# Seven half products per block pair for half of batch 6's first product, and what was moved with it

## The chip, the cores and the metric

The kernel runs on one core of one Trainium2 chip. The metric is the device time of one execution in microseconds, as the median of several runs.

## The reference

Two parts follow each other. A linear attention (cosFormer) on `q`, `k`, `v` of 8 batches, 8 heads, 576 positions, 64 features gives `x` of (8, 576, 512). Then a mixer: a low-rank mix over positions, and a two-layer product over channels.

```python
k_p = phi(k, cos_w, sin_w); q_p = phi(q, cos_w, sin_w)   # relu times cos and sin: 128 features
kv = einsum('bhsf,bhsd->bhfd', k_p, v); z = sum(k_p, axis=2)
attn = einsum('bhsf,bhfd->bhsd', q_p, kv) / (einsum('bhsf,bhf->bhs', q_p, z)[..., None] + 1e-06)
x = attn.transpose(0, 2, 1, 3).reshape(B, S, H * D)       # (8, 576, 512)
h = x.transpose(0, 2, 1) @ U @ V                          # U (576, 32), V (32, 576)
u = x + h.transpose(0, 2, 1)
out = u + maximum(u @ w_ch1, 0.0) @ w_ch2                 # w_ch1 (512, 2048), w_ch2 (2048, 512)
```

## The kernel before

**Tiling.** Per batch, 512 of the 576 positions are four chunks of 128; the other 64 are the tail, and two batches share one tail tile. All matmuls are bf16 with fp32 sums in PSUM, whose eight banks are named `g0 g1 g2 o0 o1 T` and `X` (one tile of two banks). The first product (`u @ w_ch1`, hidden width 2048 as 16 blocks of 128) is "g"; the second (`hid @ w_ch2`) is made of half products `h_ps`.

**Order.** The program is one list, `slots`. A slot is a piece of PE work: a block of the first product (`g1_main`, L566: four matmuls of 512 columns into `g0` or `g1`, then a relu on ACT), a half product (`half_part`, L853: eight matmuls of 256 columns, L882), or a quarter of a tail (`g1_tail`, L700: four blocks, 16 matmuls of 128 columns, "a tail unit"). `put(at, thunk)` hangs other work behind slot number `at`. Nothing reorders afterwards: each engine runs its own instructions in the order in which the program gave them, and waits by semaphore for what it reads or overwrites.

**Stages.** While batch b's first product runs block by block, the second product of batch b-1 is interleaved as two times seven half products (Strassen's seven for eight, with the sums `w2_sum` L789 and `hid_sum` L811), and the attention of batch b+1 is hung beside them by `attention_plan` (L991): `q_prep` and `k_prep` (ACT and DVE), `kv_unit`, five `x_unit`s (L415), `A_unit` (L452), `u_mm` (L468), four `u_add`s (L481), the transposes `utr_dma` (SP's queue), and for odd batches `u_tail` (L488). `PLAN[7]` gives 191 as the base slot of batch 7.

**x unit.** Eight matmuls fill the two banks of `X` (L422), DVE makes the reciprocal of the denominators (L412, L413) and one multiplication for all 8 heads (L432). The next x unit writes the same tile `X`.

**Batch 7's first product** uses seven products per block pair p (block p and block p+8): `g1_cross` (L647) issues product i as two matmuls of 256 columns (L670). X and Y are the halves of one bank, Z half of another; two pairs alternate over `CROSS = [("g0", "g1"), ("g2", "T")]`. The steps of a pair are

- `opened`: products 1 (X) and 2 (Y); P1 = cast of X on ACT; C11 = P1 + Y on DVE
- `second`: products 6 (onto X) and 5 (Z); casts U2 of X and P5 of Z
- `third`: product 7 (onto X); C22 = P5 + X on DVE, relu on ACT
- `closed`: products 3 (onto Z) and 4 (onto X); C12 = U2 + Z on DVE, relu of X on ACT, one relu of the upper half on DVE (L692)

It needs sums of `w_ch1` quarters (`w1_sum`, L610, in the freed tiles of `qst` and `kst`) and of the batch's transposed `u` (`uT_sum`, L631, in the freed tile of `vst`), all on DVE (L608).

**Results of the second product** of batches 5 and 6: ACT casts four of the seven half products to `o_sb`, DVE adds the others (L838), and `half_store` (L935) lets GpSimd add `u_bf` and then stores.

Of the kernel before, what the change touches and what calls it, by code (L numbers as in the profile page):

```python
# [17 lines left out]
def kernel(  # L18
# [396 lines left out]
    def x_unit(b, c, tag, bufs):  # L415
        x_alloc(b)
        n = P if c < 4 else TS
        rows = slice(0, P) if c < 4 else tail(b)
        acc = ps.tile([P, 2, 512], FP32, tag=tag, bufs=bufs, name="x_ps")
        for h in range(H):  # L420
            g, i = divmod(h, 4)
            nc.tensor.matmul(  # L422
                out=acc[:, g, i * E : i * E + E],
                lhsT=qT_of(b, c, h),
                rhs=kv_sb[b][:, h, :],
                start=(i == 0),
                stop=(i == 3),
            )
        view = acc[rows, :, 0 : 4 * E].rearrange("p g (i e) -> p g i e", e=E)
        rec = pool.tile([P, 2, 4], FP32, tag="rec", bufs=2, name="rec")  # L430
        recip(rec[rows], view[:, :, :, D])
        nc.vector.tensor_tensor(  # L432
            out=x_of(b, c, rows).rearrange("p (g i d) -> p g i d", g=2, d=D),
            in0=view[:, :, :, 0:D],
            in1=rec[rows].unsqueeze(3).to_broadcast([n, 2, 4, D]),
            op=ALU.mult,
        )

    def A_of(b):
        return A_sb[b % 4]  # L440
# [24 lines left out]

    va = {}

    def u_mm(b, *spare):  # L468
        if b not in u_bf:
            u_bf[b] = pool.tile([P, 4, 4, P], BF16, tag="u_bf", bufs=3, name="u_bf")  # L470
        va[b] = four_banks(*spare)
        for c in range(4):
            for j in range(4):
                rows = slice(j * R, j * R + R)
                nc.tensor.matmul(  # L475
                    out=va[b][j][:, c * P : c * P + P], lhsT=V_bf[rows, c, :],
                    rhs=A_of(b)[rows, :], start=(c == 0), stop=(c == 3),
                    tile_position=(j * R, 0),
                )
# [5 lines left out]
            in1=va[b][j].rearrange("p (c n) -> p c n", c=4), op=ALU.add,  # L485
        )

    def u_tail(pr, *spare):  # L488
        u_tl[pr] = pool.tile(
            [P, DM], BF16, tag="k_p" if pr == 3 else "u_tl", bufs=1, name="u_tl"  # L490
        )
        vt = four_banks(*spare)
        for i in range(2):
            for j in range(4):
                rows = slice(j * R, j * R + R)
                nc.tensor.matmul(
                    out=vt[j][tail(i), 0:P], lhsT=V_tl[rows, :],
                    rhs=A_of(2 * pr + i)[rows, :], start=True, stop=True,
                    tile_position=(j * R, i * TS),
                )  # L500
        for j in range(4):
            ns = slice(j * P, j * P + P)
            nc.vector.tensor_tensor(
                out=u_tl[pr][:, ns], in0=x_tl[:, ns], in1=vt[j][:, 0:P], op=ALU.add
            )
# [4 lines left out]

    def uTt_alloc(pr):
        if pr not in uT_tl:
            uT_tl[pr] = pool.tile([P, 4, P], BF16, tag="uT_tl", bufs=1, name="uT_tl")

    def utr_dma(b, c0, c1):
        if c0 < 4:
# [113 lines left out]

    def uT_sum(b, i):  # L631

        if i == 1:
            t = pool.tile([P, 4, 2, 2, P], BF16, tag="vst", bufs=1, name="uT_s")
            for n in range(4):
                uT_s[b, n + 1] = t[:, n]
        x, y = {
            1: lambda: (uT_quarter(b, 0, 1), uT_quarter(b, 0, 0)),
            2: lambda: (uT_quarter(b, 1, 1), uT_s[b, 1]),
            3: lambda: (uT_quarter(b, 1, 1), uT_quarter(b, 0, 1)),  # L640
            4: lambda: (uT_quarter(b, 1, 0), uT_s[b, 2]),
        }[i]()
        diff(uT_s[b, i], x, y)
# [3 lines left out]
    def g1_cross(b, p, i):  # L647

        if (b, p) not in cross:
            if b not in hid:
                hid[b] = pool.tile([P, NJ, 512], BF16, tag="hid", bufs=2, name="hid")
            xy, z = [
                psum.tile([P, 512], FP32, tag=tag, bufs=1, name="c_ps") for tag in CROSS[p % 2]
            ]
            cross[b, p] = {"X": xy[:, 0:256], "Y": xy[:, 256:512], "Z": z[:, 0:256]}
        w = cross[b, p]
        cs = slice(p * P, p * P + P)
        to, lhs, rhs, first = {  # L660
            1: lambda: ("X", W1[0], uT_quarter(b, 0, 0), True),
            2: lambda: ("Y", W1[1], uT_quarter(b, 1, 0), False),
            3: lambda: ("Z", w1_s[4], uT_quarter(b, 1, 1), False),
            4: lambda: ("X", W1[3], uT_s[b, 4], False),
            5: lambda: ("Z", w1_s[1], uT_s[b, 1], True),
            6: lambda: ("X", w1_s[2], uT_s[b, 2], False),
            7: lambda: ("X", w1_s[3], uT_s[b, 3], False),
        }[i]()
        for d in range(2):
            nc.tensor.matmul(  # L670
                out=w[to].rearrange("p (c t) -> p c t", c=2), lhsT=lhs[:, d, cs],
                rhs=rhs[:, d], start=(first and d == 0), stop=(d == 1),
                skip_group_check=not first,
            )

    def g1_join(b, p, i):
# [7 lines left out]
        if i == "C11":  # L684
            diff(top[:, lo], w["P1"], w["Y"], ALU.add)
        elif i == "C22":
            diff(low[:, hi], w["P5"], w["X"], ALU.add)
            relu(low[:, hi], low[:, hi])
        elif i == "C12":
            diff(top[:, hi], w["U2"], w["Z"], ALU.add)  # L690
            relu(low[:, lo], w["X"])
            V_.tensor_scalar(out=top, in0=top, scalar1=0.0, scalar2=None, op0=ALU.max)  # L692
        else:
            if (b, "kept") not in cross:
                cross[b, "kept"] = pool.tile([P, 2, 3, 256], FP32, tag="q_pT", bufs=1, name="kept")
            n = ("P1", "U2", "P5").index(i)
            w[i] = cross[b, "kept"][:, p % 2, n]
            cast(A_, w[i], w["Z" if i == "P5" else "X"])
# [274 lines left out]
    def spare(at):  # L973
# [11 lines left out]
        4: (100, (-20, 1, V_, V_), (-13, 2, A_, V_), -12, (-9, -4, -4)),  # L985
        5: (127, (-24, 2, A_, A_), (-14, 2, A_, V_), (-14, -8, -5), (-8, -4, -4)),
        6: (157, (-23, 2, A_, A_), (-14, 2, A_, V_), (-14, -8, -6), (-8, -4, -4)),
        7: (191, (-24, 2, A_, A_), (-14, 2, A_, V_), (-14, -12, -10), ()),
    }

    def attention_plan(b):  # L991
# [39 lines left out]
            else:  # L1031
                put(4 + (3 * n) // 2, x_unit, c, "X", 1)
        a_at = 15 - b if b < 4 else 14
        put(a_at, A_unit, tag=True)
        odd = b % 2 == 1


        def two(at):
            return [T1, ("s", 1)] if at >= 88 else [spare(at)] * 2

        plan.append((w + a_at + 2, lambda: u_mm(b, *two(w + a_at + 2))))
        for j in range(4):
            put(a_at + 2 + j + (2 if b > 4 and j > 1 else 0), u_add, j)
        put(a_at + 3, utr_dma, 0, 2)
        put(a_at + (7 if b > 4 else 5), utr_dma, 2, 4)
        if odd:
            plan.append(
                (w + a_at + 9, lambda: u_tail(b // 2, *two(w + a_at + 9)))
            )
# [283 lines left out]
    def g1(b, j):  # L1333
        return lambda: g1_main(b, j)
# [22 lines left out]
    for b in range(3, B - 1):  # L1357
# [4 lines left out]
        for n in range(2):  # L1362
            for i7 in range(7):
# [4 lines left out]
        if b % 2:  # L1368
            tail_slots(b // 2)
        if b == 3:  # L1370
            tail_out(b // 2)

    at = len(slots)
    b7 = B - 1
    for i, half, sl in (
        (1, 0, -4), (1, 1, -3), (3, 0, -3), (3, 1, -2), (2, 0, -1), (2, 1, 21), (4, 0, 22), (4, 1, 25),
    ):
        put(at - 30 + sl, lambda i=i, half=half: w1_sum(i, half))
    for i in range(4):
        put(at - 4 + i, lambda i=i: uT_sum(b7, i + 1))  # L1380
    sums(b7 - 1, 0, (at, at + 1, at + 6))
    sums(b7 - 1, 1, (at + 13, at + 15, at + 19))

    def opened(p):
        g1_cross(b7, p, 1)
        g1_cross(b7, p, 2)
        g1_join(b7, p, "P1")
        g1_join(b7, p, "C11")

    def second(p):  # L1390
        g1_cross(b7, p, 6)
        g1_cross(b7, p, 5)
        g1_join(b7, p, "U2")
        g1_join(b7, p, "P5")

    def third(p):
        g1_cross(b7, p, 7)
        g1_join(b7, p, "C22")

    def closed(p):  # L1400
        g1_cross(b7, p, 3)
        g1_cross(b7, p, 4)
        g1_join(b7, p, "C12")

    def group(p, first, then):
        def go():
            if p < 8:
                first(p)
            if p > 0:
                then(p - 1)  # L1410

        return go

    groups = [
        group(p, *fs) for p in range(9) for fs in ((opened, third), (second, closed))
    ]
    halfs = [(n, i7) for n in range(2) for i7 in range(7)]
# [8 lines left out]
    for i, go in enumerate(groups):  # L1426
        slots.append(go)
        if i < 14:
            n, i7 = halfs[i]
            slots.append(lambda n=n, i7=i7: half_part(b7 - 1, n, i7, "with g"))  # L1430
            if i7 > 4:
                put(len(slots), lambda n=n, i7=i7: half_store(b7 - 1, n, i7 - 5))
        else:
            slots.append(lambda j=i - 14: tail_cross(j))
    at = len(slots)
# [76 lines left out]
```

## Time and profile before

| | |
|---|---|
| median of 3 runs | 294.66 us (294.53 to 294.97) |
| profiled execution | 294.26 us, span of its instructions 292.5 us |
| PE busy | 284.3 us, 97% of the span |
| DVE, ACT, GpSimd busy | 203.6, 166.9, 55.8 us |
| granted TensorE clock | 0.998 |
| 210.58 to 240.19 us (batch 6's first product) | PE 29.35, DVE 19.40, ACT 13.41, POOL 5.54 us busy |
| 240.19 to 243.66 us (start of batch 7's) | PE 2.78, DVE 3.40, ACT 1.92, POOL 2.09 us busy |

A row of the timeline gives start, duration, engine, line, operation, what it writes and reads, and in brackets the idle time ahead of it with what ended it. Rows of one engine that overlap are counted once in busy times. A group's row gives busy time, the mean of one in ns, and the idle time ahead of the group with its releasers. The chain of waits names, for each stretch of the span, what the end of the program hung on.

### The profile page before, as it was taken

Reading aid. Unit: us, or ns where it says so; the run is one execution under the profiler, and the core shown is the slowest. Engines: PE = TensorE matmul, PEld = TensorE weight load, DVE = VectorE, ACT = ScalarE, POOL = GpSimd, SP = SyncE. Lnnn points to the kernel's source line nnn. Section 1 sums busy time; section 2 is a strip of 40 time slices with the busy share of each in tenths; the row PEclk is TensorE's granted clock in tenths of the full one; section 3 lists DMA queues with packets and bytes.
Section 4 is the critical chain, followed back from the end, with each engine's and each line's share of the span. In section 5 each row is a group of like instructions: output and inputs, shape, how many; then the busy total and the mean of one; then the engine's idle time right before and its main releaser. Section 6 shows DMA issues by size and latency. Waiting matters only on the chain.

```text
span 292.5 us, 7212 instructions
## 1 busy us (share of the span) xinstructions
PE 284.3 (97%) x2884; PEld 191.8 (66%) x2920; DVE 203.6 (70%) x484; ACT 166.9 (57%) x340; POOL 55.8 (19%) x92
## 2 busy tenths in 40 slices
PE   8999999999999999999999999999999999999994
PEld 4675564447545446676767667766776667889883
DVE  5977855496875697556547793778827687865773
ACT  2955742276882767577736765298753445567210
POOL 6520500000020004202300501040202331302330
PEclk9999999999999999999999999999999999999999
DMA  7999999999998989998799939974800321101023
GB/s 226 304 254 251 275 160 222 205 318 228 340 194 175 294 212 259 240 315 237 147 250 265 242 88 280 231 266 92 215 0 4 110 68 59 50 24 72 2 94 125
DMA packets 90949, 54.07 MB, mean 185 GB/s; under 512 B 58564, under 2 KB 87620, under 8 KB 90916
## 3 DMA queue, kind: packets, MB, share of 16 engines
q1 hardware_dynamic: 84420, 43.94, 60.2%
q0 software_dynamic: 6304, 9.47, 14.6%
q8 instruction: 23, 0.38, 0.5%
q10 hardware_dynamic: 192, 0.20, 0.2%
q14 instruction: 10, 0.08, 0.1%
HBM read 36.86 MB, written 9.44 MB: 158 GB/s over the span
## 4 chain that ended last, share of the span: by engine, by line
PE 90%; DMA 3%; ACT 2%; DVE 2%; issue 1%; ACTq 0%; DVEq 0%
PE g_ps L576 31%; PE h_ps L882 26%; PE o_ps L750 11%; PE gt_ps L710 5%; PE c_ps L670 4%; PE kv_ps L347 3%; PE x_ps L422 3%; DMA qst<-in_q_dram 2%; DVE uT_s L608 1%; PE a_ps L445 1%; PE h_ps L750 1%; PE g_ps L593 1%; DMA uT<-u_bf 1%; PE va_ps L475 1%; PE t_ps L365 1%
## 5 line engine op out<-in xcount | busy, mean ns | idle before, releaser
L576 PE MATMUL g_ps<-uT,w_bf 128*128 128x512 bf16 x408 | 103.5, 379 | 1.3
L585 ACT ACTIVATE hid<-g_ps 128x512 bf16<-128x512 f32 x112 | 65.8, 599 | 64.2 <-PE g_ps L576 63.8
L576 PEld LDWEIGHTS <-w_bf 128*128 128x128 bf16 x434 | 40.9, 98 | 36.7
L882 PEld LDWEIGHTS <-hid 128*128 128x128 bf16 x480 | 45.4, 98 | 9.6
L882 PE MATMUL h_ps<-w_bf,hid 128*128 128x256 bf16 x288 | 37.1, 273 | 0.0
L750 PE MATMUL o_ps<-w_bf,hid 128*128 128x512 bf16 x122 | 29.4, 379 | 0.4 <-issue 0.2
L882 PE MATMUL h_ps<-w_s,S 128*128 128x256 bf16 x208 | 26.5, 273 | 0.0
L131 POOL CAST v_ext<-vst 128x512 bf16<-128x512 f32 (+1 forms) x23 | 15.2, 687 | 57.4 <-DMA vst<-in_v_dram 26.8
L838 DVE TENSOR_TENSOR o_sb<-o_sb,h_ps 128x256 f32<-128x256 f32 (+1 forms) x36 | 15.5, 433 | 15.1 <-PE h_ps L882 9.9
L882 PE MATMUL h_ps<-w_s,hid 128*128 128x256 bf16 x192 | 24.9, 273 | 0.0
L483 DVE TENSOR_TENSOR u_bf<-x_bf,va_ps 128x512 bf16<-128x512 bf16 x27 | 17.7, 680 | 8.3 <-PE va_ps L475 4.7
L838 POOL TENSOR_TENSOR o_sb<-o_sb,u_bf 128x512 f32<-128x512 f32 x10 | 12.1, 1205 | 57.5 <-DVE o_sb L838 43.8
L882 PEld LDWEIGHTS <-S 128*128 128x128 bf16 x208 | 19.9, 98 | 4.4
L838 DVE TENSOR_TENSOR o_sb<-u_bf,h_ps 128x256 f32<-128x256 bf16 x28 | 11.7, 417 | 14.3 <-PE h_ps L882 14.2
L941 POOL DMA_DIRECT2D out_dram<-o_sb x16 | 9.9, 619 | 54.0 <-DVE o_sb L838 51.2
L750 PEld LDWEIGHTS <-hid 128*128 128x128 bf16 x128 | 11.5, 98 | 12.2
L710 PE MATMUL gt_ps<-uT_tl,w_bf 128*128 128x128 bf16 x256 | 16.1, 219 | 0.0
L432 DVE TENSOR_TENSOR x_bf<-x_ps,rec 128x512 bf16<-128x512 f32 x22 | 15.2, 691 | 0.8
L710 PEld LDWEIGHTS <-w_bf 128*128 128x128 bf16 x256 | 14.9, 98 | 0.8
L306 ACT ACTIVATE k_p<-kst,cosw 128x512 bf16<-128x512 f32 x20 | 14.2, 713 | 0.1
L608 DVE TENSOR_TENSOR hid<-kept,c_ps 128x256 bf16<-128x256 f32 x24 | 9.4, 418 | 6.6 <-PE c_ps L670 3.5
L306 ACT ACTIVATE q_p<-qst,sinw 128x512 bf16<-128x512 f32 x18 | 12.6, 709 | 1.7 <-DMA qst<-in_q_dram 1.7
(188 smaller groups left out, 429.0 us busy)
## 6 DMA issues: line engine op xcount, KB each, us to landing
qst<-in_q_dram SPq DMA_DIRECT2D x14, 512.0 KB, 6.0
kst<-in_k_dram SPq DMA_DIRECT2D x14, 512.0 KB, 6.6
vst<-in_v_dram SPq DMA_DIRECT2D x12, 512.0 KB, 6.8
out_dram<-o_sb POOLq DMA_DIRECT2D x19, 256.0 KB, 3.7
out_dram<-o_sb SPq DMA_DIRECT2D x16, 256.0 KB, 2.5
w_bf<-in_moe_w_ch_dram POOLq DMA_DIRECT2D x7, 512.0 KB, 13.7
qst<-in_q_dram SPq DMA_DIRECT2D x2, 640.0 KB, 13.1
kst<-in_k_dram SPq DMA_DIRECT2D x2, 640.0 KB, 7.1
```

The costliest lines, as they stand in the source:

```text
L131: eng.tensor_copy(out=o, in_=i)
L306: nc.scalar.activation(out=o, in_=i, func=AF.Relu, bias=0.0, scale=w)
L432: nc.vector.tensor_tensor(out=x_of(b, c, rows).rearrange("p (g i d) -> p g i d", g=2, d=D), in0=view[:, :, :, 0:D], in1=rec[rows].unsqueez ...
L483: nc.vector.tensor_tensor(out=u_bf[b][:, j, :, :], in0=x_bf[b][:, :, ns], in1=va[b][j].rearrange("p (c n) -> p c n", c=4), op=ALU.add,)
L576: nc.tensor.matmul(out=g_ps.rearrange("p (c t) -> p c t", c=4), lhsT=w1_bf[:, d, j * P : j * P + P], rhs=uT[b][:, d, :, :], start=(d == 0) ...
L585: nc.scalar.activation(out=hid[b][:, j, :], in_=g_ps, func=AF.Relu, bias=0.0, scale=1.0)
L608: V_.tensor_tensor(out=o, in0=x, in1=y, op=op)
L670: nc.tensor.matmul(out=w[to].rearrange("p (c t) -> p c t", c=2), lhsT=lhs[:, d, cs], rhs=rhs[:, d], start=(first and d == 0), stop=(d == 1 ...
L710: nc.tensor.matmul(out=g_ps[:, jj, :], lhsT=w1_bf[:, d, j * P : j * P + P], rhs=uT_tl[pr][:, d, :], start=(d == 0), stop=(d == 3),)
L750: nc.tensor.matmul(out=o[:, cols], lhsT=lhs[:, j, c * P : c * P + P], rhs=w2_bf[:, j, cols], start=(j == 0), stop=(j == NJ - 1),)
L838: eng.tensor_tensor(out=o, in0=x, in1=y, op=ALU.add)
L882: nc.tensor.matmul(out=acc, lhsT=lhs[:, j, :], rhs=rhs[:, j, :], start=(j == 0 and at is not None), stop=(j == 7), skip_group_check=at is ...
```

## The change

1. For batch 6, block pairs 4 to 7 of the first product are made by the seven products; pairs 0 to 3 stay plain. Three banks serve: X and Y of a pair in `g0` or `g1` in turn, and one bank `T` for Z, its halves in turn. `kept` lies in the tile of `q_p`. Batch 6 gets its own four `uT_s` sums.
2. Of the four tail units of pair 2, two stay before batch 6's first product; units 2 and 3 come behind it, in the two banks of `X`. Batch 7's base slot goes from 191 to 189 (its `qtr_dma` keep their slots).
3. As `T` is taken, `u_mm` and `u_tail` of batch 7 are cut: three of four column groups first, the fourth later, alone in `X`.
4. In batch 7's x units of the four chunks DVE does heads 0 to 3, ACT heads 4 to 7 (four scalings); batch 7's `A_sb` cast goes from DVE to ACT, its bank from the tagged one to `g2`.
5. The halves of `w1_sum` get other slots: six ahead of batch 6's first product (before five), two within it (before three).
6. The `half_store`s of batch 5's second half are put eight and nine slots later.

```diff
@@ x_unit
+        gs = 1 if b == B - 1 and c < 4 else 2
         nc.vector.tensor_tensor(
-            out=x_of(b, c, rows).rearrange("p (g i d) -> p g i d", g=2, d=D),
...
+        for i in range(4 * (2 - gs)):
+            nc.scalar.activation(
+                out=x_of(b, c)[:, (4 + i) * D : (5 + i) * D], in_=view[:, 1, i, 0:D],
+                func=AF.Copy, bias=0.0, scale=rec[:, 1, i : i + 1],
+            )
@@ u_mm (u_tail alike)
-    def u_mm(b, *spare):
+    def u_mm(b, *spare, js=range(4)):
-        va[b] = four_banks(*spare)
+        va.setdefault(b, {}).update(zip(js, four_banks(*spare)))
         for c in range(4):
-            for j in range(4):
+            for j in js:
@@ g1_cross
+            if b < B - 1:
+                if "Z" not in cross:
+                    cross["Z"] = psum.tile([P, 512], FP32, tag="T", bufs=1, name="z_ps")
+                xy = psum.tile([P, 512], FP32, tag=("g0", "g1")[p % 2], bufs=1, name="c_ps")
+                z = cross["Z"][:, 256 * (p % 2) : 256 * (p % 2) + 256]
@@ PLAN, attention_plan
-        7: (191, (-24, 2, A_, A_), (-14, 2, A_, V_), (-14, -12, -10), ()),
+        7: (189, (-24, 2, A_, A_), (-14, 2, A_, V_), (-12, -10, -8), ()),
+        if b == B - 1:
+            put(a_at, A_unit, "s", 1, A_)
...
+            plan.append((w + a_at + 2, lambda: u_mm(b, ("s", 1), js=(0, 1, 2))))
+            plan.append((w + a_at + 4, lambda: u_mm(b, js=(3,))))
...
+                plan.append((w + a_at + 9, lambda: u_tail(b // 2, ("s", 1), js=(0, 1, 2))))
+                plan.append((w + a_at + 10, lambda: u_tail(b // 2, js=(3,))))
@@ the slots of batch 6's first product
+        elif b % 2:
+            slots.extend(lambda pr=b // 2, j=j: g1_tail(pr, j) for j in range(2))
...
+    def beside_g(b, m):
+        n, i7 = halfs[m]
+        slots.append(lambda: half_part(b, n, i7, "with g"))
+        if i7 > 4:
+            later = {5: 8, 6: 9}[i7] if (b, n) == (b6 - 1, 1) else 0
+            put(len(slots) + later, lambda: half_store(b, n, i7 - 5))
...
     for i, half, sl in (
-        (1, 0, -4), (1, 1, -3), (3, 0, -3), (3, 1, -2), (2, 0, -1), (2, 1, 21), (4, 0, 22), (4, 1, 25),
+        (1, 1, -8), (2, 1, -6), (3, 1, -4), (1, 0, -3), (4, 1, -2), (3, 0, -1), (2, 0, 11), (4, 0, 23),
     ):
-        put(at - 30 + sl, lambda i=i, half=half: w1_sum(i, half))
+        put(at + sl, lambda i=i, half=half: w1_sum(i, half))
+    for i in range(4):
+        put(at + 1 + i, lambda i=i: uT_sum(b6, i + 1))
+    units = [g1(b6, j) for p in range(3) for j in (p, p + 8)] + [g1(b6, 3)]
+    units.append(lambda: [g1_main(b6, 11), opened(b6, 4)])
+    units.append(crossed((second, b6, 4)))
+    for p in range(5, 8):
+        units.append(crossed((opened, b6, p), (third, b6, p - 1)))
+        units.append(crossed((closed, b6, p - 1), (second, b6, p)))
+    units.append(crossed((third, b6, 7)))
+    slots += units[0:2]
+    for m in range(14):
+        beside_g(b6 - 1, m)
+        slots.append(units[2 + m])
...
+    slots.append(lambda: tail_late(2))
+    slots.append(crossed((closed, b6, 7)))
+    slots.append(lambda: tail_late(3))
```

More of the change, by code (lines that the diff above doesn't have):

```diff
@@ L431, in x_unit @@
         recip(rec[rows], view[:, :, :, D])
+        gs = 1 if b == B - 1 and c < 4 else 2
         nc.vector.tensor_tensor(
-            out=x_of(b, c, rows).rearrange("p (g i d) -> p g i d", g=2, d=D),
-            in0=view[:, :, :, 0:D],
-            in1=rec[rows].unsqueeze(3).to_broadcast([n, 2, 4, D]),
+            out=x_of(b, c, rows)[:, 0 : gs * 256].rearrange("p (g i d) -> p g i d", g=gs, d=D),
+            in0=view[:, 0:gs, :, 0:D],
+            in1=rec[rows, 0:gs].unsqueeze(3).to_broadcast([n, gs, 4, D]),
             op=ALU.mult,
         )
+        for i in range(4 * (2 - gs)):
[3 more added lines that the diff above has]
+            )
     def A_of(b):
@@ L486, in u_add, with u_tail @@
         )
[L488 to L492, printed above, removed]
+    def u_tail(pr, *spare, js=range(4)):
+        if pr not in u_tl:
+            u_tl[pr] = pool.tile(
+                [P, DM], BF16, tag="k_p" if pr == 3 else "u_tl", bufs=1, name="u_tl"
+            )
+        vt = dict(zip(js, four_banks(*spare)))
         for i in range(2):
-            for j in range(4):
+            for j in js:
                 rows = slice(j * R, j * R + R)
@@ L500, in u_tail @@
                 )
-        for j in range(4):
+        for j in js:
             ns = slice(j * P, j * P + P)
@@ L512, in uTt_alloc @@
         if pr not in uT_tl:
-            uT_tl[pr] = pool.tile([P, 4, P], BF16, tag="uT_tl", bufs=1, name="uT_tl")
+            uT_tl[pr] = pool.tile(
+                [P, 4, P], BF16, tag="x_bf" if pr == 3 else "uT_tl", bufs=1, name="uT_tl"
+            )
     def utr_dma(b, c0, c1):
@@ L631, in uT_sum @@
     def uT_sum(b, i):
-        if i == 1:
-            t = pool.tile([P, 4, 2, 2, P], BF16, tag="vst", bufs=1, name="uT_s")
+        if not uT_s:
+            t = pool.tile([P, 2, 4, 2, 2, P], BF16, tag="vst", bufs=1, name="uT_s")
             for n in range(4):
-                uT_s[b, n + 1] = t[:, n]
+                for m in range(2):
+                    uT_s[B - 2 + m, n + 1] = t[:, m, n]
         x, y = {
@@ L653, in g1_cross @@
                 hid[b] = pool.tile([P, NJ, 512], BF16, tag="hid", bufs=2, name="hid")
-            xy, z = [
-                psum.tile([P, 512], FP32, tag=tag, bufs=1, name="c_ps") for tag in CROSS[p % 2]
-            ]
+            if b < B - 1:
[3 more added lines that the diff above has]
+                z = cross["Z"][:, 256 * (p % 2) : 256 * (p % 2) + 256]
+            else:
+                xy, z = [
+                    psum.tile([P, 512], FP32, tag=tag, bufs=1, name="c_ps")
+                    for tag in CROSS[p % 2]
+                ]
             cross[b, p] = {"X": xy[:, 0:256], "Y": xy[:, 256:512], "Z": z[:, 0:256]}
@@ L694, in g1_join @@
             if (b, "kept") not in cross:
-                cross[b, "kept"] = pool.tile([P, 2, 3, 256], FP32, tag="q_pT", bufs=1, name="kept")
+                cross[b, "kept"] = pool.tile(
+                    [P, 2, 3, 256], FP32, tag="q_pT" if b == B - 1 else "q_p", bufs=1,
+                    name="kept",
+                )
             n = ("P1", "U2", "P5").index(i)
@@ L1033, in attention_plan @@
         a_at = 15 - b if b < 4 else 14
[L1034 removed]
+        if b == B - 1:
+            put(a_at, A_unit, "s", 1, A_)
+        else:
+            put(a_at, A_unit, tag=True)
         odd = b % 2 == 1
@@ L1039, in two @@
             return [T1, ("s", 1)] if at >= 88 else [spare(at)] * 2
-        plan.append((w + a_at + 2, lambda: u_mm(b, *two(w + a_at + 2))))
+        if b == B - 1:
+            plan.append((w + a_at + 2, lambda: u_mm(b, ("s", 1), js=(0, 1, 2))))
+            plan.append((w + a_at + 4, lambda: u_mm(b, js=(3,))))
+        else:
+            plan.append((w + a_at + 2, lambda: u_mm(b, *two(w + a_at + 2))))
         for j in range(4):
@@ L1046, in attention_plan @@
         if odd:
-            plan.append(
-                (w + a_at + 9, lambda: u_tail(b // 2, *two(w + a_at + 9)))
-            )
+            if b == B - 1:
+                plan.append((w + a_at + 9, lambda: u_tail(b // 2, ("s", 1), js=(0, 1, 2))))
+                plan.append((w + a_at + 10, lambda: u_tail(b // 2, js=(3,))))
+            else:
+                plan.append((w + a_at + 9, lambda: u_tail(b // 2, *two(w + a_at + 9))))
             put(a_at + 10, utr_dma, 4, 5)
@@ L1356 @@
     alone = len(slots)
-    for b in range(3, B - 1):
+    for b in range(3, B - 2):
         at = len(slots)
@@ L1367, with opened, second @@
                 slots.append(g1(b, 2 + 7 * n + i7))
-        if b % 2:
+        if b == 3:
             tail_slots(b // 2)
-        if b == 3:
             tail_out(b // 2)
+        elif b % 2:
+            slots.extend(lambda pr=b // 2, j=j: g1_tail(pr, j) for j in range(2))
+    b6, b7 = B - 2, B - 1
+    def opened(b, p):
+        g1_cross(b, p, 1)
+        g1_cross(b, p, 2)
+        g1_join(b, p, "P1")
+        g1_join(b, p, "C11")
+    def second(b, p):
+        g1_cross(b, p, 6)
+        g1_cross(b, p, 5)
+        g1_join(b, p, "U2")
+        g1_join(b, p, "P5")
@@ new lines, in third, with closed, crossed, go @@
+    def third(b, p):
+        g1_cross(b, p, 7)
+        g1_join(b, p, "C22")
+    def closed(b, p):
+        g1_cross(b, p, 3)
+        g1_cross(b, p, 4)
+        g1_join(b, p, "C12")
+    def crossed(*steps):
+        def go():
+            for f, b, p in steps:
+                f(b, p)
+        return go
+    halfs = [(n, i7) for n in range(2) for i7 in range(7)]
+    def beside_g(b, m):
[4 more added lines that the diff above has]
+            put(len(slots) + later, lambda: half_store(b, n, i7 - 5))
@@ L1373 @@
     at = len(slots)
-    b7 = B - 1
+    sums(b6 - 1, 0, (at, at + 1, at + 3))
+    sums(b6 - 1, 1, (at + 13, at + 15, at + 19))
     for i, half, sl in (
-        (1, 0, -4), (1, 1, -3), (3, 0, -3), (3, 1, -2), (2, 0, -1), (2, 1, 21), (4, 0, 22), (4, 1, 25),
+        (1, 1, -8), (2, 1, -6), (3, 1, -4), (1, 0, -3), (4, 1, -2), (3, 0, -1), (2, 0, 11), (4, 0, 23),
     ):
-        put(at - 30 + sl, lambda i=i, half=half: w1_sum(i, half))
+        put(at + sl, lambda i=i, half=half: w1_sum(i, half))
@@ L1379, with tail_late @@
+    tail23 = {}
+    def tail_late(j):
+        if j == 2:
+            tail23["t"] = ps.tile([P, 2, 512], FP32, tag="X", bufs=1, name="gt_ps")
+        g1_tail(2, j, tail23["t"][:, j - 2, :].rearrange("p (j t) -> p j t", j=4))
+    slots.append(lambda: tail_late(2))
+    slots.append(crossed((closed, b6, 7)))
+    slots.append(lambda: tail_late(3))
+    at = len(slots)
     for i in range(4):
         put(at - 4 + i, lambda i=i: uT_sum(b7, i + 1))
-    sums(b7 - 1, 0, (at, at + 1, at + 6))
-    sums(b7 - 1, 1, (at + 13, at + 15, at + 19))
@@ L1384, in opened @@
[L1384 to L1403, printed above, removed]
-    def group(p, first, then):
[L1406 to L1412, printed above, removed]
+    sums(b6, 0, (at, at + 1, at + 6))
@@ L1414 @@
+    sums(b6, 1, (at + 13, at + 15, at + 19))
+    def group(p, first, then):
+        return crossed(*([(first, b7, p)] if p < 8 else []), *([(then, b7, p - 1)] if p else []))
     groups = [
@@ L1416 @@
     ]
-    halfs = [(n, i7) for n in range(2) for i7 in range(7)]
     def tail_cross(j):
@@ L1428 @@
         if i < 14:
[L1429 to L1432, printed above, removed]
+            beside_g(b6, i)
         else:
```

## The prediction

> **What bounds the kernel now.** I read the page's busy shares first, then its chain, then the chain in order of time from 205 to 275 us, the timeline of 199 to 250 us, and last the groups by form for the prices.
>
> ```profile
> PE 284.3 (97%) x2884; PEld 191.8 (66%) x2920; DVE 203.6 (70%) x484; ACT 166.9 (57%) x340; POOL 55.8 (19%) x92
> PE 90%; DMA 3%; ACT 2%; DVE 2%; issue 1%; ACTq 0%; DVEq 0%
> ```
>
> PE sets the end, so work that PE no longer does is gained only if PE gets no new gap. The chain in order of time shows the stage that the change rebuilds (first product of batch 6, 210.58 to 240.19 us, "stage 6") and the handover to batch 7 ("stage 7"):
>
> ```profile
> 210.58 0.22 PE g_ps L576
> ...
> 226.09 0.86 PE g_ps L576 x4
> 226.96 0.39 PE a_ps L445 x20
> 227.35 0.98 PE h_ps L882 x8
> ...
> 235.25 2.73 DMA uT<-u_bf
> ...
> 238.58 3.39 DVE uT_s L608 x3
> 241.97 0.34 DVE hid L608
> 242.31 0.04 issue
> 242.35 0.60 PE c_ps L670 x4
> ```
>
> Up to 234 us the pieces are all PE's: sixteen blocks of 0.87, fourteen half products of 0.87, and the attention units of batch 7 fill 29.6 us without a gap. At the handover the chain leaves PE: `u_bf`'s transpose, the four `uT_s` sums, a join, then PE at 242.35. The half product before it began at 240.62 and issues for 0.87, to 241.49: PE lost 0.86 there. Why the sums were late stands in the timeline:
>
> ```profile
> 238.30 1.26 POOL L838 TENSOR_TENSOR o_sb<-o_sb,u_bf 128x512 f32<-128x512 f32 x1 [8.93 <-DVE o_sb L838]
> 238.58 1.26 DVE L608 TENSOR_TENSOR uT_s<-uT,uT_s 128x512 bf16<-128x512 bf16 x1
> 240.10 1.87 DVE L608 TENSOR_TENSOR uT_s<-uT,uT_s 128x512 bf16<-128x512 bf16 x1
> 240.50 1.17 POOL L838 TENSOR_TENSOR o_sb<-o_sb,u_bf 128x512 f32<-128x512 f32 x1
> ```
>
> A sum of 0.42 alone took 1.26 and 1.87, and both ended 0.3 after a GpSimd add. Prices come from these groups:
>
> ```profile
> L1288 ACT ACTIVATE x_bf<-x_ps,rec 128x64 bf16<-128x64 f32 x24 | 5.5, 325 | 7.7 <-DVE rec L412 7.6
> L483 DVE TENSOR_TENSOR u_bf<-x_bf,va_ps 128x512 bf16<-128x512 bf16 x27 | 17.7, 680 | 8.3 <-PE va_ps L475 4.7 <-PE side L475 2.3 <-ACT hid L585 1.3
> L608 DVE TENSOR_TENSOR hid<-kept,c_ps 128x256 bf16<-128x256 f32 x24 | 9.4, 418 | 6.6 <-PE c_ps L670 3.5 <-ACT kept L129 3.1
> ```
>
> Back to back they cost less than their durations, because they overlap: by their starts in the timeline, 0.60 for a DVE operation of 0.68, 0.33 for one of 0.42, 0.27 for an ACT cast of 0.38, 0.49 for the 0.60 relu, and 0.205 for a 64-wide ACT scaling (eight took 1.75). A reader starts 0.20 after PE's last matmul is issued; PE resumes 0.05 after a DVE or ACT result.
>
> **Gains.** Four block pairs go from 8 matmuls of 512 columns (two pieces of 0.867, 1.73) to 14 of 256 (8 in 0.87, so 1.52): 0.21 each, 0.86. Tail units 2 and 3 (0.93 each: all four took 3.73 from 206.85) only change place, but now stand between the last `uT` transposes and stage 7. `u_bf` is done early enough for them to cover the transpose's 2.73 and most of the sums, so the 0.86 gap goes, down to 0.05. Together 1.67.
>
> **Costs.** They are waits, found by laying the built program's instruction order (each wait names its instruction) against these prices. T is the end of the `opened(4)` step.
>
> 1. x units. ACT now scales heads 4 to 7. It waits for DVE's half of the same unit, and the next unit's matmuls into tile X wait for ACT. From a unit's start: matmuls to 0.26, `rec` 0.46, reciprocal 0.66, DVE half (L1089 form, 0.41) 0.89 to 1.29, scalings 1.37 to 2.30. PE returns to X after 0.26 + 0.87 + 0.87 = 2.00 and stands until 2.35. Twice (the third has `opened(4)` between): 0.70. Below: 0, if the rows overlap more; above: 0.9.
>
> 2. A unit. It moves from behind a 0.87 block to behind `second(4)`, 0.43. DVE's queue before it: C11(4) waits for the P1 cast, which stands behind a relu on ACT (relu from T-0.23, cast T+0.26 to 0.64), so C11 starts at T+0.72; then a `hid` sum (T+1.05), `rec` (1.65), reciprocal, DVE half of x (2.09 to 2.49), ACT scalings (2.57 to 3.50). PE: x unit to T+0.26, half product to 1.13, `second(4)` held by C11 to 1.19, then to 1.62, 16 A matmuls to 1.93, and the last wait for 3.55. Stall 1.6, and 0.1 at `second(4)`. Bounds 1.0 (without the sum ahead) and 2.1.
>
> 3. The shared Z bank. Product 5 of pair p+1 waits for C12(p), since both halves of Z are one bank. PE has only products 4 and 6 in between after product 3 (0.65 from the half product's end to product 5); DVE is in order. For pair 5 it must, after the half product ends, do its `o_sb` add (from +0.20), `u_add` 1 (+0.53), a `hid` sum (+1.13), C12 (+1.73 to +2.15): PE starts at +2.20, stall 1.55. For pair 6, from the end e of `opened(6)`: PE has product 7, a half product, products 3, 4 and 6, to e+1.74; DVE has C11(6) from e+0.50 (its cast ends at 0.42), C22 0.83, `u_add` 2 and 3 at 1.16 and 1.76, C12 2.36 to 2.78: stall 1.1. For pair 7: one `o_sb` add and C12, ready at 1.00 against 0.65: 0.35. Sum 3.0; bounds 2.2 and 3.6 (one 0.60 operation more or less, with a little). Behind the waiting product on PE stand the A and U matmuls and every later half product; for them wait `u_add` and the transposes.
>
> Before, `c_ps` has one row of this kind, 0.69 behind `DVE hid`: X and Y of a pair share a bank, and a write into X waits for a read of Y. The Trainium skill ("PSUM — Partial Sum Buffer", bank collisions) says to guard PSUM by bank and not by address. By addresses alone the 3.0 would fall away. Row and rule agree against the change.
>
> 4. Late tail units. Unit 3 writes the two-bank tile that ACT still reads for unit 2: 0.20 + 0.60 + 0.05 against 0.43 of products 3 and 4, so 0.4; the split tail matmuls of `u_tail` wait 0.1 for two adds. Sum 0.5 (0.2 to 0.7).
>
> Covered: the six early `w_ch1` sums (0.60 each) and batch 6's first `hid` sums end by about 211 us on DVE, and the first half product that needs one starts at 215.4; without that cover each costs 0.6. Preparation of batch 7 moves two slots earlier on ACT and DVE: `qst` had landed at about 184, and its first use moves from 190.4 to 188.7. SP's order is unchanged; its `uT` transposes land 5 us before need. The moved GpSimd adds still wait only for their own `o_sb`, and nothing in the program holds them until the later slot, so I give that move nothing either way.
>
> Sum: 0.7 + 1.6 + 0.1 + 3.0 + 0.5 = 5.9 lost, 1.67 gained, +4.2. The profiled execution took 294.26 (span 292.5), so 298.5; that is 0.4 under the median of 294.66, which goes to 298.9.
>
> **Rivals.**
> Faster: DVE and ACT keep up and PE sees none of these waits. For it: DVE is busy 19.4 of 29.6 us in stage 6, ACT 13.4, and before no gap shows there. Against: an average hides an in-order queue that has to answer within 0.65. Time 294.66 - 1.7 = 292.9; it decides if the new gaps sum to less than 1.7.
> No change: the gaps come to 1.1 to 2.3, the time to 294.1 to 295.2.
> Slower by less: DVE runs ahead in the gaps it causes, and terms 1 to 4 go to their low ends, 0 + 1.0 + 2.2 + 0.2 = 3.4, so +1.7 and 296.4.
> Slower by more: the two adds of batch 5's second half start after the last `o_sb` steps, right where the `uT_s` sums of batch 7 are due. If they hold DVE there as in the rows above (1.26 - 0.42 and 1.87 - 0.42, 2.3 in all) and 0.6 of it is covered, it is +5.9 and 300.6. The Trainium skill ("SBUF — State Buffer", Who interferes with whom) calls the port that DVE's two-input operations share with GpSimd an exclusive lock. The stretched rows agree.
> The change doesn't do what it says: the GpSimd adds do not move at all, as above; that is in the forecast.
>
> **How the numbers follow.** Forecast 0.70, less slow 0.12, slower by more 0.07, faster 0.07, no change 0.04. The range goes from the low ends (296.4) to the more-case with a little above (300.8). A measurement of this kernel can tell about 0.2%, 0.6 us, from no change. Faster 0.07, same 0.04, slower 0.89.
>
> **What would show it.** PE gaps in the timeline at the second and third x unit (0.35), before the last A matmul (1.6, released by ACT `x_bf`), before product 5 of pairs 5 to 7 (1.55, 1.1, 0.35, released by DVE `hid`), before the last late tail unit (0.4). The handover gap of 0.86 should be near zero, and the tail of the kernel (from stage 7's second pair on) should last as long as before. I am wrong if product 5 starts without a gap, or if the stretch from batch 6's first block to the second `opened` of stage 7 (before 210.58 to 243.66, 33.1) takes under 36 us, where 33.1 + 1.9 (the moved tails) - 1.7 + 5.9 = 39.2 is forecast.

## The result and the profile after

The changed kernel takes 299.88 us in the median of 6 runs (299.57 to 300.95); the kernel before, beside it on the same chip, took 294.68. The ratio is 1.0174, with a 95% interval of 1.0152 to 1.0197: slower by 5.2 us, where 4.2 were forecast. The profiled execution took 299.85 us with a span of 298.1, which is 5.6 above the span of before; the terms below are held against that 5.6. In the text TensorE, VectorE, ScalarE and GpSimd are the PE, DVE, ACT and POOL of the rows.

The busy shares and the chain's shares, of the page after:

```profile
PE 288.3 (97%) x2944; PEld 194.5 (65%) x2944; DVE 209.1 (70%) x503; ACT 172.4 (58%) x369; POOL 55.0 (18%) x92
PE 86%; DVE 5%; ACT 4%; DMA 2%; issue 1%; ACTq 0%; DVEq 0%
```

TensorE's share stands at 97% as before, so the busy line tells almost nothing. The second line does: TensorE carries 86% of the chain, before it was 90%; VectorE and ScalarE together have gone from 4% to 9%. The work that sets the end now leaves TensorE at several places. Which ones, TensorE's waits between 208 and 250 us say (what waited, for whom: us in total, how often, the longest):

```profile
PE z_ps L687 <- DVE hid L617: 2.6, 3, 1.5
PE a_ps L451 <- ACT x_bf L440: 0.6, 2, 0.4
PE x_ps L422 <- ACT x_bf L440: 0.5, 2, 0.2
PE a_ps L451 <- DVE x_bf L433: 0.4, 1, 0.4
PE gt_ps L730 <- ACT hid_tl L737: 0.2, 1, 0.2
```

In the same view before there was one row, 0.7 of `c_ps` behind `hid` at the handover; it is gone. This view counts from the modelled end of the last matmul, so each wait costs TensorE's queue some 0.1 to 0.2 more than it shows. Counted from issue to issue, as the forecast did, the timeline gives the price: eight matmuls of 256 columns take 0.87, two take 0.22, and what lies between the end of that and the next start is lost. The rows of the longest waits:

```profile
219.52 0.42 PE L422 MATMUL x_ps<-kv,q_pT 128*128 128x65 bf16 x8 [0.24 <-ACT x_bf L440]
227.92 0.22 PE L451 MATMUL a_ps<-x_bf,U_bf 128*32 128x128 bf16 x1 [0.19 <-ACT x_bf L440]
231.36 0.38 PE L687 MATMUL c_ps<-uT_s,w_s 128*128 128x256 bf16 x2
233.27 0.38 PE L687 MATMUL z_ps<-uT_s,w_s 128*128 128x256 bf16 x2 [1.53 <-DVE hid L617]
...
236.93 0.38 PE L687 MATMUL c_ps<-uT_s,w_s 128*128 128x256 bf16 x2
238.23 0.38 PE L687 MATMUL z_ps<-uT_s,w_s 128*128 128x256 bf16 x2 [0.93 <-DVE hid L617]
```

Where the chain left TensorE for the longest time, in order of time:

```profile
224.61 0.42 ACT kept L129
...
225.05 0.42 DVE hid L617
225.47 0.60 DVE S L844
226.07 0.09 DVE rec L412
...
226.19 0.21 DVE rec L413
...
226.42 0.43 DVE x_bf L433
...
226.94 0.94 ACT x_bf L440 x4
...
227.92 0.22 PE a_ps L451
...
230.76 0.60 DVE u_bf L489
231.36 0.33 DVE o_sb L858
231.69 0.60 DVE u_bf L489
232.28 0.60 DVE hid L844
232.89 0.34 DVE hid L617
...
233.27 0.38 PE z_ps L687 x2
```

The first half is `A_unit` standing behind the whole row of cast, C11, `hid` sum, reciprocal, multiplication and four scalings: its 20 matmuls hold TensorE from 226.05 to 228.07, 2.02 where they took 0.39 before. The second half is the shared Z bank: product 5 of pair 5 waits until VectorE has done two `u_add`s, an `o_sb` add and a `hid` sum and has read C12 out of the other half of that bank.

### The profile page after: what moved, and what is told of

It reads as the page before. It is cut to its first block, busy times and chain, and to the rows that moved or that the text cites. A ratio compares the mean times of both kernels' runs of the same rounds, so it can differ in the third digit from the quotient of the medians.

```text
span 298.1 us, 7359 instructions
## 1 busy us (share of the span) xinstructions
PE 288.3 (97%) x2944; PEld 194.5 (65%) x2944; DVE 209.1 (70%) x503; ACT 172.4 (58%) x369; POOL 55.0 (18%) x92
## 4 chain that ended last, share of the span: by engine, by line
PE 86%; DVE 5%; ACT 4%; DMA 2%; issue 1%; ACTq 0%; DVEq 0%
PE g_ps L585 28%; PE h_ps L902 25%; PE o_ps L770 10%; PE c_ps L687 5%; PE gt_ps L730 4%; PE kv_ps L347 3%; PE x_ps L422 3%; DMA qst<-in_q_dram 2%; ACT x_bf L440 1%; DVE hid L617 1%; PE h_ps L770 1%; PE a_ps L451 1%; PE g_ps L602 1%; DVE uT_s L617 1%; DVE x_bf L433 1%
## 5 line engine op out<-in xcount | busy, mean ns | idle before, releaser
L585 PE MATMUL g_ps<-uT,w_bf 128*128 128x512 bf16 x402 | 97.3, 379 | 0.0
L594 ACT ACTIVATE hid<-g_ps 128x512 bf16<-128x512 f32 x104 | 61.1, 600 | 53.7 <-PE g_ps L585 53.0
L585 PEld LDWEIGHTS <-w_bf 128*128 128x128 bf16 x402 | 37.7, 98 | 34.6 <-DMA w_bf<-in_moe_w_ch_dram 0.3
L770 PE MATMUL o_ps<-w_bf,hid 128*128 128x512 bf16 x128 | 30.1, 379 | 0.0
L617 DVE TENSOR_TENSOR hid<-kept,c_ps 128x256 bf16<-128x256 f32 x32 | 12.6, 418 | 13.0 <-ACT kept L129 8.8
L730 PEld LDWEIGHTS <-w_bf 128*128 128x128 bf16 x256 | 15.1, 98 | 1.1 <-issue 0.4
L433 DVE TENSOR_TENSOR x_bf<-x_ps,rec 128x512 bf16<-128x512 f32 (+1 forms) x22 | 14.1, 643 | 0.8
L129 ACT ACTIVATE kept<-c_ps 128x256 f32<-128x256 f32 x32 | 11.4, 382 | 4.7 <-PE c_ps L687 4.2
```

The source lines that it names most:

```text
L433: nc.vector.tensor_tensor(out=x_of(b, c, rows)[:, 0 : gs * 256].rearrange("p (g i d) -> p g i d", g=gs, d=D), in0=view[:, 0:gs, :, 0:D], i ...
L585: nc.tensor.matmul(out=g_ps.rearrange("p (c t) -> p c t", c=4), lhsT=w1_bf[:, d, j * P : j * P + P], rhs=uT[b][:, d, :, :], start=(d == 0) ...
L594: nc.scalar.activation(out=hid[b][:, j, :], in_=g_ps, func=AF.Relu, bias=0.0, scale=1.0)
L617: V_.tensor_tensor(out=o, in0=x, in1=y, op=op)
L730: nc.tensor.matmul(out=g_ps[:, jj, :], lhsT=w1_bf[:, d, j * P : j * P + P], rhs=uT_tl[pr][:, d, :], start=(d == 0), stop=(d == 3),)
L770: nc.tensor.matmul(out=o[:, cols], lhsT=lhs[:, j, c * P : c * P + P], rhs=w2_bf[:, j, cols], start=(j == 0), stop=(j == NJ - 1),)
```

## The experiments

In the expectations "before" is the kernel before, run beside the experiment on the same chip. All kernels below but e3, e6, e9 and e11 start from the changed one. The chips differ between experiments, so a difference between two of them is given by their medians and, where it matters, also by their ratios to before. Two profiles can also differ ahead of batch 6's first block, where the kernels do the same: by 0.78 between before and e6 (210.41 and 211.19). Where traces are compared, the count starts at that block.

**e1: x units wholly on VectorE.**

```diff
-        gs = 1 if b == B - 1 and c < 4 else 2
+        gs = 2
```

> The changed kernel (299.88 us), with batch 7's x units wholly on DVE again; the A_sb cast stays on ACT. Theory of waits: the two gaps of 0.39 before the second and third x unit go, and the wait of the last A matmuls shrinks from 1.55 to about 0.8, because one DVE multiplication of 0.69 takes the place of 0.42 on DVE and then 0.93 on ACT: 1.5 less, 298.4 us. Rival (the half products themselves cost more, waits are a symptom): no change, 299.9 us.

Measured: 298.48 us, ratio 1.0131 (1.0118 to 1.0144). Against the changed kernel that is 1.3 us won back by the ratios, 1.4 by the medians. The rows of `x_ps` waiting for `x_bf` are gone, and `A_unit` has one gap instead of three; TensorE's timeline of e1:

```profile
226.59 0.24 PE L451 MATMUL a_ps<-x_bf,U_bf 128*32 128x128 bf16 x4 [0.70 <-DVE x_bf L433]
231.96 0.38 PE L687 MATMUL z_ps<-uT_s,w_s 128*128 128x256 bf16 x2 [1.53 <-DVE hid L617]
```

So the split of the multiplication costs all of term 1 (0.78 measured) and a little under half of term 2: `A_unit` still holds TensorE 0.90 too long (225.47 to 226.76, less 0.39) where it was 1.63, behind C11 and the `hid` sum, and 0.23 comes back ahead of `second(4)`. The Z wait next to it has not changed at all (1.53 in both).

**e2: a second bank for Z.** Odd pairs put Z in `g2`; for that, V times A is cut in two and two column groups.

```diff
...
-                z = cross["Z"][:, 256 * (p % 2) : 256 * (p % 2) + 256]
+                z = psum.tile([P, 512], FP32, tag=("T", "g2")[p % 2], bufs=1, name="z_ps")
...
```

> The changed kernel, with a bank of its own for Z of the odd pairs (g2); to free it, u_mm and u_tail of batch 7 are cut two and two within X, the second halves one slot later. Theory of waits: product 5 no longer waits for C12, so the gaps of 1.69, 1.08 and 0.35 go, 3.1 in all; the cut two and two costs up to 0.3 in other places: 296.8 to 297.2 us. Rival (the half products themselves cost more): 299.9 us. A second rival: DVE is simply full, so the 3.1 comes back as gaps at other joins, 299 to 300 us.

Measured: 296.89 us, ratio 1.0084 (1.0069 to 1.0099): by the medians 3.0 won back, by the ratios 2.7; from batch 6's first block to the end of the span it is 86.3 (from 209.29) where the changed kernel took 89.4 (from 208.66), so 3.1. No `z_ps` row is left among TensorE's waits; product 5 of pair 5 (`z_ps`) follows product 6 (`c_ps`) at its normal pace, 0.22 later:

```profile
231.98 0.38 PE L685 MATMUL c_ps<-uT_s,w_s 128*128 128x256 bf16 x2
232.20 0.38 PE L685 MATMUL z_ps<-uT_s,w_s 128*128 128x256 bf16 x2
```

VectorE's queue holds the same operations in both kernels, so the queue alone does not cost the 3.1: it costs because TensorE has to wait for a read of the other half of the bank. A full VectorE, the second rival, would have brought the gaps back elsewhere; only the handover grew, from 0.27 to 0.39. Whether the wait belongs to the bank or to the tile that held both halves is not shown, as e2 separates both at once.

**e3 and e9: the late tail units alone**, in the kernel before (batch 7's base slot at 189, `uT_tl` of pair 3 in the tile of `x_bf`).

```diff
+        elif b % 2:
+            slots.extend(lambda pr=b // 2, j=j: g1_tail(pr, j) for j in range(2))
...
+    slots.append(lambda: g1_tail(2, 2))
+    slots.append(tail_x)
```

> The kernel before, with the late tail units alone: two of pair 2's four tail units stand behind batch 6's first product (one in the g banks, one in X), batch 7's base slot 189, uT_tl of pair 3 in the freed x_bf. All blocks plain. Theory of waits: the handover gap of 0.86 shrinks to 0.0 to 0.3, nothing else changes: 293.8 to 294.1 us. Rival (the gap is set by the GpSimd adds that stretch the uT_s sums, and moves along with them): 294.7 us.

> e3 again, the kernel before with nothing but the two late tail units, on the same chip as e8: 0.86 of gap is gone in its trace and 0.5 was measured. If that is real: 293.8 to 294.3 beside a before of 294.7, ratio 0.997 to 0.999. If it was scatter: 294.7.

Measured: e3 294.19 us, ratio 0.9989 (0.9972 to 1.0006), not to be told from no change; e9, the same kernel on another chip, 293.86 against 294.39, ratio 0.998 (0.9969 to 0.999). The second shows a gain of 0.5 to 0.6 (0.3 to 0.9 by its interval), and this part alone is faster than before and computes the whole result, which no other version here does. TensorE's timeline of e3 at the handover:

```profile
238.24 1.95 PE L712 MATMUL gt_ps<-uT_tl,w_bf 128*128 128x128 bf16 x32
240.02 0.60 PE L672 MATMUL c_ps<-uT,w_bf 128*128 128x256 bf16 x4
240.46 1.04 PE L884 MATMUL h_ps<-w_bf,hid 128*128 128x256 bf16 x8
241.60 0.60 PE L672 MATMUL c_ps<-uT_s,w_s 128*128 128x256 bf16 x4
```

The half product of 0.87 ends its issue at 241.33, `second` follows at 241.60. The gap is 0.27, not 0.05: of before's 0.86 only 0.59 could be won, and 0.5 to 0.6 was.

**e4: the stores of batch 5's second half not moved.**

```diff
-            later = {5: 8, 6: 9}[i7] if (b, n) == (b6 - 1, 1) else 0
+            later = 0
```

> The changed kernel, with the half_stores of batch 5's second half in their old slots. Theory: the later slot holds nothing, GpSimd starts its adds when o_sb is done, in both; the same time within 0.2 us, 299.9, and the adds start within 0.3 us of the same o_sb rows. Rival (the later slot keeps the adds away from DVE's sums): slower by 0.5 to 1.5 us, 300.4 to 301.4.

Measured: 300.23 us, ratio 1.0194 (1.0174 to 1.0214), beside the changed kernel's 1.0174; the intervals overlap. GpSimd's rows decide, of e4:

```profile
242.75 1.15 POOL L858 TENSOR_TENSOR o_sb<-o_sb,u_bf 128x512 f32<-128x512 f32 x1 [11.91 <-DVE o_sb L858]
```

and of the changed kernel:

```profile
242.22 1.15 POOL L858 TENSOR_TENSOR o_sb<-o_sb,u_bf 128x512 f32<-128x512 f32 x1 [11.91 <-DVE o_sb L858]
```

In both the add starts 0.3 ahead of pair 7's product 5 (243.05 and 242.51), released by the same VectorE add. Eight slots later in the program is no later on a queue that had been idle for 11.91 us.

**e5: plain blocks.** All 16 blocks of batch 6 in 512 columns, everything else as changed; tail unit 3 in bank `T`.

```diff
...
+    units += [g1(b6, 11)] + [g1(b6, j) for p in range(4, 8) for j in (p, p + 8)]
...
```

> The changed kernel with the four last block pairs of batch 6 as plain 512-column blocks again, so without half products in batch 6 and without their waits; the late tail units, the x units split between VectorE and ScalarE, the moved sums and the two-part cut of V times A stay (the sums uT_s of batch 6 are still made and not used), and tail unit 3 has a bank of its own. If the waits are the cost: the handover gap is gone (about -0.5 as the late tails alone gave it, -0.9 by the trace of before), three x units wait 0.39 each (+1.2), the cut costs 0.5, A_unit waits about 0.1: +0.8 to +1.3 on before, 295.5 to 296.0. If the half products in themselves cost what the changed kernel lost (more instructions, tile switches, weight loads) and the waits only mirror that: the kernel is at or under before, 293.9 to 294.7.

Measured: 295.97 us against 294.74, ratio 1.007 (1.0041 to 1.0099), span 294.1. TensorE's waits between 208 and 245 us:

```profile
PE x_ps L422 <- ACT x_bf L440: 0.7, 3, 0.2
PE va_ps L481 <- DVE u_bf L489: 0.3, 1, 0.3
```

The first row was expected. The second was not: the second part of V times A writes the two banks that the first part's `u_add`s still read. In the changed kernel the 1.69 at Z stands in front of it and hides it. By issue times: x units 1.18, A 0.13, cut 0.50, this wait 0.38, less 0.59 at the handover, together 1.60; the spans differ by 1.6. So what was moved beside the half products is a loss by itself. The half products with their waits, and tail unit 3's 0.41, cost 3.9 on top by the medians (295.97 to 299.88), 3.1 by the ratios (e5's interval is wide).

**e6: the cut of V times A alone**, in the kernel before.

```diff
...
+            plan.append((w + a_at + 2, lambda: u_mm(b, ("s", 1), js=(0, 1, 2))))
+            plan.append((w + a_at + 4, lambda: u_mm(b, js=(3,))))
...
```

> The kernel before with one edit: batch 7's V times A as 12 matmuls of three column groups and, two slots later, the 4 of the last group, in place of all 16 at once. If matmuls of one 32-row group queue behind each other, and four groups run side by side, the part of 4 costs as much as the 16 did (0.33): 295.0. If it costs by its share of the matmuls, or is hidden: 0.08 or nothing, 294.7 to 294.8. A difference of 0.3 is near what five rounds can tell, so the PE row of the trace decides: 0.33 against 0.08 for the 4 matmuls.

Measured: 296.13 us against 294.74, ratio 1.0031 (1.0001 to 1.0062), more than either expectation, with a wide interval. TensorE's timeline of before, one row, and of e6:

```profile
229.12 0.40 PE L475 MATMUL va_ps<-A_sb,V_bf 32*128 32x128 bf16 x16
```

```profile
229.90 0.40 PE L475 MATMUL va_ps<-A_sb,V_bf 32*128 32x128 bf16 x12
230.24 1.05 PE L882 MATMUL h_ps<-w_bf,hid 128*128 128x256 bf16 x8
231.12 1.03 PE L576 MATMUL g_ps<-uT,w_bf 128*128 128x512 bf16 x4
232.45 0.39 PE L475 MATMUL va_ps<-A_sb,V_bf 32*128 32x128 bf16 x4 [0.31 <-DVE u_bf L483]
232.78 1.05 PE L882 MATMUL h_ps<-w_s,S 128*128 128x256 bf16 x8
```

From start to the next row's start: 12 matmuls 0.34, the last 4 take 0.33, and before all 16 took 0.34 (229.12 to 229.46). Each column group is made in its own 32 rows of TensorE's array (`rows` in `u_mm`), so four matmuls of one row group cost as much as sixteen in four. Ahead of the 4 stands the wait of e5. Both together are 0.7, within the interval; the profile's span is 1.5 longer than before's, and the other 0.8 lies ahead of batch 6's first block, where nothing was edited.

**e7: three waits taken away.** e1 and e2 together, the late tail unit 3 in `T`, and

```diff
-    sums(b6 - 1, 1, (at + 13, at + 15, at + 19))
+    sums(b6 - 1, 1, (at + 15, at + 17, at + 19))
```

> The changed kernel with its three waits taken away together: x units wholly on VectorE, a bank of its own for the third product group of the odd pairs, the late tail unit 3 in another bank than unit 2, and the hid sums of batch 5 two slots later so that they stand behind the x unit's multiply. Cut of V times A (0.5) and half products stay. If waits and cut are the whole loss: before 294.7, less 0.86 for the half products, less 0.5 for the handover, plus 0.5 for the cut and 0.2 to 0.6 of waits that are left at the handover and at A_unit: 294.0 to 294.5. If the half products have a cost that no wait shows, it stays over 295.5.

Measured: 295.63 us against 294.74, ratio 1.0036 (1.0016 to 1.0055): 4.2 of the 5.2 came back by the medians, but not below before, where 294.0 to 294.5 was expected: a miss. TensorE's timeline of e7 at the handover shows why:

```profile
241.88 0.60 PE L685 MATMUL c_ps<-uT,w_bf 128*128 128x256 bf16 x4
242.31 1.04 PE L900 MATMUL h_ps<-w_bf,hid 128*128 128x256 bf16 x8
244.01 0.60 PE L685 MATMUL c_ps<-uT_s,w_s 128*128 128x256 bf16 x4 [0.65 <-DVE hid L617]
```

242.31 + 0.87 = 243.18, so 0.83 is lost: the gap of before is back, now that TensorE comes there sooner. Two reasons were left, a VectorE queue that is too long or GpSimd's adds. At `A_unit`, with the `hid` sum out of its way, TensorE is held only 0.30, so that sum was the larger part of e1's 0.90.

**e8: e7 with a shorter queue.**

```diff
...
-(2, 0, 11), (4, 0, 23),
+(2, 0, 11), (4, 0, 13),
...
```

> e7 with one sum of first-layer weights (the second half product's sum of index 4, 0.69 on VectorE) ten slots earlier, into a stretch where VectorE stood idle for over 0.8, out of the queue that runs without a pause up to the handover to batch 7. If the 0.83 that TensorE stands at the handover in e7 is VectorE's queue being too long there, it falls by about 0.6: a gap of 0.2 to 0.3, and 295.0 where e7 had 295.6. If the gap is set by GpSimd's adds stretching the sums beside them, whatever else is queued, it stays over 0.7 and the time stays.

Measured: 296.38 us, ratio 1.0065 (1.0048 to 1.0082): worse. With 0.6 less in the queue the handover gap is still 0.70, so the queue's length gives 0.13 of the 0.83 at most; and in its new place the sum lies ahead of the x unit that `A_unit` waits for, which then holds TensorE 0.6 longer than in e7. (Another 0.57 of e8's profile lies ahead of batch 6's first block, 209.73 against e7's 209.16, and so ahead of the edit.)

**e10 and e11: the two GpSimd adds left out**, in e7 and in the kernel before.

```diff
-        if b in LENT:
+        if b in LENT and (b, n) != (B - 3, 1):
```

> e7 with two GpSimd adds left out, those of u for the two last stores of batch 5 (output rows of that batch miss u; the stores stay). They run from 238.3 to 241.5 in e7's trace, beside the sums uT_s on VectorE. If they set the 0.83 that TensorE stands at the handover, the first uT_s sum takes 0.4 in place of 1.57 and the gap falls to 0.2 or less: 295.0 where e7 had 295.6. If VectorE's queue is too long there anyway, the gap stays over 0.6.

> The kernel before with the same two GpSimd adds left out (the same output rows miss u). If they stretch the uT_s sums that TensorE waits for at the handover (1.26 and 1.87 where others of the form take 0.42), both fall to 0.42 and the gap of 0.86 goes: 293.8 to 294.0 beside 294.7. If the sums are late for another reason (the DMAs that bring their input), the gap stays.

Both kernels leave out a part of the result. Measured: e10 294.99 us against 295.01, ratio 1.0012 (0.9999 to 1.0026); e11 294.05, ratio 0.9968 (0.9957 to 0.998). TensorE's timeline of e11:

```profile
240.99 1.04 PE L882 MATMUL h_ps<-w_bf,hid 128*128 128x256 bf16 x8
242.13 0.60 PE L670 MATMUL c_ps<-uT_s,w_s 128*128 128x256 bf16 x4
```

and VectorE's, with the two sums that took 1.26 and 1.87 before:

```profile
238.94 0.43 DVE L608 TENSOR_TENSOR uT_s<-uT,uT_s 128x512 bf16<-128x512 bf16 x1
239.62 0.42 DVE L608 TENSOR_TENSOR uT_s<-uT,uT_s 128x512 bf16<-128x512 bf16 x1
```

Without the adds all four sums take 0.42 to 0.43, and the gap is 0.27 in e11 (242.13 less 240.99 and 0.87; before it was 0.86) and 0.28 in e10 (from 0.83). GpSimd's adds set the handover gap in both. What is left, 0.27, is another chain: `opened`, its cast on ScalarE, C11, `second`, with only one half product between. In e11 C11 starts 1.11 after `opened`; in e3, in e10 and in the changed kernel it is within 0.01 of that.

## Why the prediction was right, and where it was off

The sign, the place and the mechanism of each large cost held: e1 and e7 show it for terms 1 and 2, e2 for term 3. TensorE's gaps in the changed kernel, from issue to issue:

| term | forecast | measured |
|---|---|---|
| 1. x units, second and third of the chunks | 0.70 | 0.39 + 0.39 |
| 2. `A_unit`; at `second(4)` | 1.6; 0.1 | 1.63; 0.06 |
| 3. Z bank, pairs 5, 6, 7 | 1.55, 1.1, 0.35 | 1.69, 1.08, 0.35; product 4 of pair 5 0.17 |
| 4. late tail unit 3; `u_tail`'s second part | 0.4; 0.1 | 0.41; 0.18 |
| cut of V times A and of `u_tail` | not priced | 0.33 + 0.17 |
| half products | -0.86 | -0.86 |
| handover | -0.81 | -0.59 |
| sum | +4.2 | +5.4, spans +5.6 |

Two terms carry 0.7 of the 1.2 us by which the two sums differ.

*The cut was not priced.* The prediction spoke of the split tail matmuls' wait for adds, but took for granted that 12 + 4 matmuls cost what 16 did. They cost 0.67 (e6, and 0.33 + 0.33 in the changed kernel), the cut `u_tail` 0.19 + 0.17 for 0.19. The Trainium skill ("TensorE: Matmul & The Clock Gate", Why this matters for your kernels) says that small matmuls in distinct row groups run at the same time, and that the gain is this concurrency. The rows agree, 16 in 0.34 against 4 of one group in 0.33; taking one group out of four therefore saves nothing (12 still take 0.34) and adds a whole pass.

*The handover gain was oversized.* "Down to 0.05" overlooked that with the sums out of the way the next late thing is `opened`'s own cast and join, 0.27 after the half product. The prediction put the 0.05 in which TensorE resumes where a chain of three engines stood. That the late tail units hide the stretched sums did hold: in e3 the two sums still take 1.26 and 1.86, but end 1.1 before C11 needs VectorE.

The small rest: pair 5's Z wait is 0.14 longer because the `o_sb` add that begins VectorE's chain starts 0.37 after the half product and not 0.20: two joins and a `u_add` ahead of it could begin only at 230.01, behind a cast. Product 4 of pair 5 waits 0.17 for C22, seen by no step.

The signs that the prediction named came out. From batch 6's first block to the second `opened` of stage 7 it is 208.66 to 249.34, 40.7 us, where 39.2 were forecast and under 36 would have refuted it. (The 210.58 that it took for before is the chain's; by the timeline the block starts at 210.41, so 0.2 of the difference is in the reading.) From there to the end of the span it is 48.8 in both kernels.

The rivals: *Faster* and *no change* needed gaps under 2.3; they are 6.85 with the cut. *Slower by less* had 2.2 for the Z bank and 1.0 for A; the trace puts the first at 3.12, of which e2 wins back 2.7 to 3.1, and the second at 1.63. *Slower by more* had a mechanism that is real but did not decide. In the changed kernel the adds stretch two VectorE operations there:

```profile
242.49 1.02 DVE L709 TENSOR_SCALAR hid<-hid 128x512 bf16<-128x512 bf16 x1
244.43 1.34 DVE L617 TENSOR_TENSOR uT_s<-uT 128x512 bf16<-128x512 bf16 x1
```

TensorE comes to the handover so late, after the other waits, that C11 still starts on time, 1.11 after `opened`: the last `uT_s` sum ends at 247.56, the cast that C11 needs at 247.53. That is luck and not design, by some hundredths of a microsecond, and the prediction did not see it. The measured 299.88 is near that rival's 300.6 by the cut and the 0.27 at the handover, not by the adds. In e7, where TensorE comes sooner, the same adds cost 0.56. *The change doesn't do what it says* holds for its sixth part: the adds do not move (e4).

What stays open: whether the half products pay once every wait is gone. e10 against e11, both without the adds, is 294.99 against 294.05. In e10's trace 0.28 ahead of `second(4)`, 0.30 at `A_unit`, 0.44 ahead of pair 5's product 4, 0.19 ahead of the second part of V times A and 0.5 for the cut still stand against the 0.86 that the half products save; that is 0.85 lost, near the 0.94 measured. No version here was free of these.

## What to carry to other kernels

In this program a product that wrote half of a PSUM bank waited for whoever read the other half, with everything that stood ahead of that read in the reader's queue; so a method that saved 0.86 us of matmuls and shared a bank to do it lost 3.1. Before cutting a group of small matmuls that run side by side, price the remainder as a whole group, and look whether its bank is free yet. When a wait is removed, work out the chain that is late next: a removed gap falls to that chain, not to zero, and a gap thought removed comes back (e7) when the engine arrives sooner.

## What the runs showed of the hardware

- GpSimd's adds stretch VectorE's one-input bf16 operation in SBUF as well (0.29 to 1.02 at 242.49 in the changed kernel, to 0.63 in e7), not only sums of two inputs; the stretched operation ended 0.14 after the add (243.37), the `uT_s` sum 0.29 after its add (245.48). A join that reads PSUM kept its 0.42 in e7 (238.50) though it lay wholly beside an add (238.28 to 239.43).
- Two column groups of V times A, 8 matmuls, also take 0.33 in e2: with one, two, three or four groups the time is that of four matmuls in a row.
